# Other issuing engines for some loads and stores, and another written-out instruction order, in a fused gated recurrence and MLP kernel

## Chip, cores and metric

The kernel runs on one core of one Trainium2 chip. The metric is device time in microseconds (us) of one execution; all arithmetic is in float32 except where raw bits are moved.

## The reference

There are two parts. The first is a gated linear recurrence with batch 4, 8 heads, 768 time steps and head width 48; the second is a per-token MLP with a residual, on the heads laid side by side (384 wide).

```python
f = 1.0 / (1.0 + np.exp(-f_logit))
for t in range(S):
    state = f[:, :, t, :, None] * state + np.einsum('bhd,bhe->bhde', k[:, :, t], v[:, :, t])
    y[:, :, t] = np.einsum('bhd,bhde->bhe', q[:, :, t], state)
x = y.transpose(0, 2, 1, 3).reshape(B, S, H * D)
xn = (x - mean(x)) / np.sqrt(var(x) + 1e-06) * g_ln
out = x + np.maximum(xn @ w_ch1, 0.0) @ w_ch2        # w_ch1: 384 x 1536, w_ch2: 1536 x 384
```

## The kernel before

**Units.** The 768 steps are cut into 12 units of 64 steps, all four batches at once. A unit's 256 tokens lie as two groups g of 128 rows. Units 0 and 1 of the MLP use plain matmuls; from unit 2 the second matrix product is a seven-product block scheme (`pp`, L1025), and from unit 3 the first one is a 15-product block scheme (`by_blocks`; banks `bw`, `bx`, `bv`, `by`, `bz`, L931).

**Attention stages of a unit n**, each a token `a{n}.stage` in an order string: `gates` (sigmoid of f on ScalarE, L685 or L689), `after` and `upto` (products of gates as scans on VectorE, L658 and L670), `k` and `q` (VectorE products with the gates into `kh` and `qh`, L677 or L706 and L715), `kept` (state by total gate, L724), `carried` (L738), `scores` (L752), `causal` (mask on VectorE, L758), `kt`, `values` (L787, then copies into `x`, L796 and L798), `stats`, `norm` (L855), `turn` (transposes into `xt`, L866 and L868), `chunk` (L825) and `state` (L833).

**Transposed inputs.** Units 0 to 2 transpose f, k and q on TensorE (`tr`, L650; `kp`, L778 for kh). From unit 3 on ("direct") this is done by DMA: `split` (token `p`) packs one group of f, q, k or kh (written K) into 16-bit halves with a ScalarE copy (`planes`, L433, two buffers) and sends 256 KB of it to DRAM (`halves`, L437); `transfer` (token `x`) and `kt` bring it back with a transposing DMA issued by SyncE (L452).

**Loads.** `load` (token `l`) issues one 96 KB DMA for each batch, so four for a unit's f, k, q or v (two with a trailing group digit), on SyncE's queue (L464). Weights arrive as int64 words in 12 pieces of 768 KB: `f` issues the DMA (L526), `r` splits words on ScalarE (L538, L539), `w` rebuilds the float bits on VectorE (L547, L550, L552) and adds on GpSimd (L554). `T` and `t` mix blocks of the second matrix (L577), `u` and `U` blocks of the first (L603); capitals are on GpSimd. `d` is an idle matmul (L568).

**Order.** Nothing is scheduled by a planner. `START` is one written list for units 0 to 2 of the MLP and the attention of units 0 to 4; `UNIT` is repeated for m = 3 to 11 with n = m+1, o = m+2, p = m+3, z = m+4. Each engine and each queue executes its instructions in the order in which the list issues them. A token `m{m}` advances the MLP of unit m by one step: in a repeated unit, 15 steps of `by_blocks` and then seven `pp` products (p1, p2, p6, p5, p7, p3, p4). `s{m}` makes the block sums that p6, p5, p7 and p3 read (L910 to L913), `y{n}` those for the next unit's `by_blocks` (L901). Single PSUM banks come from a pool of four. `h00` and `h01` advance the first matrix product of unit 0 for each group (L880).

Semaphores of DMAs come from eight lanes used in turn by SyncE's and ScalarE's queues, so a DMA can wait for an earlier one in its lane to land, whichever of the two queues that one is on.

Of the kernel before, what the change touches and what calls it, by code (L numbers as in the profile page):

```python
# [299 lines left out]


START = """
l0q0 d a0.gates0 d l0k0 f a0.kx0 l0f1 a0.after0 a0.carried a0.upto0 l0q1 a0.k0 l0v0
a0.q0 r a0.gates1 l0k1 f l0v1 a0.scores0 w d a0.kx1 a0.after1 a0.causal0 a0.values0
a0.k1 f a0.upto1 d a0.stats0 f l1f f d r a0.q1 w a0.kt l1k a0.scores1 d a0.norm0
a0.causal1 r a0.turn0 a0.values1 r h00 w h00 a1.gates a0.chunk a0.stats1 d r f h00 w l1q
a0.norm1 a1.after a1.upto a1.kx a0.turn1 h01 h01 l1v w a0.state h01 h00 l2f a1.q a1.kept
r w h01 f r a1.k f l2k h00 h01 r a1.carried a1.scores a1.causal h01 f a1.values a1.kt w
f a1.stats h00 r f d a1.chunk a1.norm a2.gates d a1.turn a2.kx w r m1 m1 m1 l3f w l2v w
f r r a1.state p3f0 w w m1 a2.after l3v l2q a2.k l3k p3f1 u m0 m0 m1 p3k0 a2.upto a2.kt  # L310
a2.kept l4f T x3f m0 a2.q p3k1 m0 a2.carried U l3q x3k a2.scores U p4f1 a3.gates
a2.causal t m0 a3.after p3q0 a2.chunk a2.values U m0 p3q1 l4k a2.stats p4k0 u x3q p4f0
m1 a2.state u l5f a2.norm m1 u m1 u u a2.turn a3.k m1 a3.upto a3.q p3K0 x4f p3K1 p4k1 m2
a3.kept u l4q m2 x4k u m2 a3.carried p4q1 a4.gates t a3.kt p4q0 a3.scores m2 a4.after
l5k x4q p5f0 p5f1 m1 m2 a3.causal l4v a4.upto a4.k m2 m1 p5k0 a3.values a3.chunk s2 m2 U
a3.stats m1 m2 a4.q m2 p5k1 a3.norm x5f l5q m2 p4K1 l6f a3.turn p4K0 a5.gates a3.state
m2 l5v y3 a4.kept m2 m2 U
"""
UNIT = """
a{n}.kt a{o}.after m{m} m{m} p{o}q0 m{m} m{m} m{m} a{n}.carried p{o}q1 x{o}k a{n}.scores  # L320
a{n}.causal m{m} m{m} a{n}.values m{m} x{o}q p{p}f0 a{o}.upto m{m} l{p}k a{n}.stats m{m}
m{m} p{p}f1 m{m} m{m} a{n}.norm m{m} m{m} s{m} a{o}.q l{z}f a{n}.turn x{p}f a{n}.chunk
a{n}.state m{m} p{p}k1 m{m} m{m} p{p}k0 a{o}.k l{p}q m{m} y{n} m{m} p{o}K0 p{o}K1 m{m}
a{p}.gates l{p}v m{m} a{o}.kept
"""


# [1 line left out]
def kernel(  # L329
# [19 lines left out]
    nc = tc.nc  # L349
    B, H, S, D = q.shape  # L350
    P = 128
    T = 64
# [48 lines left out]
    for name, fill in (("f", 40.0), ("q", 0.0), ("k", 0.0)):  # L401
        t = consts.tile([P, G, H, 64], FP32, name=f"{name}raw")
# [9 lines left out]
    halved = {}  # L412

    def raw_of(n, name):

        return wide_heads["k" if n >= DIRECT and name == "q" else name]
# [3 lines left out]
    def whole(n, name):  # L420
        if name != "K":
            return raw_of(n, name)
        return by_gates[n].rearrange("p (g s) t -> p g s t", g=G)

    def split(n, name, g):

        if n >= NU or n < DIRECT:
            return
        if (n, name) not in halved:
            halved[n, name] = drams.tile([P, 2, G, 64 * H], U16, tag=f"{name}halves",  # L430
                                         name=f"{name}halves{n}")
        planes = raws.tile([P, 2, 64 * H], U16, tag="planes", name=f"{name}planes{n}_{g}")
        nc.scalar.copy(  # L433
            out=planes,
            in_=whole(n, name)[:, g].rearrange("p h e -> p (h e)").bitcast(U16).rearrange(
                "p (c two) -> p two c", two=2))
        nc.gpsimd.dma_start(out=halved[n, name][:, :, g], in_=planes)  # L437

    def transfer(n, name):

        if n >= NU or n < DIRECT:
            return
        if not turned:
            turned["k"] = wide_heads["q"].rearrange("p g h e -> p (g h e)").rearrange(
                "p (s t) -> p s t", t=T)
            turned["f"] = turned["q"] = work.tile([P, NS, T], FP32, name="turned")
        transposed(turned[name].rearrange("p (g s) t -> p g (s t)", g=G), n, name)
# [7 lines left out]
    def load(n, name, gs=range(B // 2), engines=(nc.sync,)):  # L455
        if n >= NU:
            return
        if name != "v":
            loaded[n, name] = raw_of(n, name)
        elif (n, name) not in loaded:  # L460
            loaded[n, name] = raws.tile([P, G, H, D], FP32, tag="rawv", name=f"v{n}")
        src = {"f": f_logit, "k": k, "q": q, "v": v}[name]
        for b in (b for b in range(B) if b // 2 in gs):
            engines[b % len(engines)].dma_start(  # L464
                out=loaded[n, name][(b % 2) * T:(b % 2 + 1) * T, b // 2, :, 0:D],
                in_=src[b, :, n * T:(n + 1) * T, :].rearrange("h p d -> p h d"))
# [40 lines left out]
    def pieces(dst, src, name, by_rows):  # L507
        rows, cols = dst.shape[1], dst.shape[2]
        sv = src.rearrange("(c p) f -> p c f", p=P)
        r, w = (PIECE // cols, cols) if by_rows else (rows, PIECE // rows)  # L510
        return [(f"{name}{i}_{j}", sv[:, i:i + r, j:j + w], dst[:, i:i + r, j:j + w], r, w)
                for i in range(0, rows, r) for j in range(0, cols, w)]

    queue = pieces(w1, moe_w_ch1, "w1", False) + pieces(w2, moe_w_ch2, "w2", True)
# [356 lines left out]
    def first_half(n, g):  # L871
        xt = xt_of[n]
        if n not in h_of:
            h_of[n] = work.tile([P, KF, W], FP32, tag="h", bufs=2, name=f"h{n}")
        h, tokens = h_of[n], slice(g * P, (g + 1) * P)
        for i in range(0, KF, 2):
            ph = one_bank(f"ph{n}")[:, 0:2 * P].rearrange("p (i t) -> p i t", i=2)
            for j in range(2):
                for m in range(KD):
                    nc.tensor.matmul(ph[:, j], lhsT=w1[:, m, (i + j) * P:(i + j + 1) * P],  # L880
                                     rhs=xt[:, m, tokens], start=m == 0, stop=m == KD - 1)
            nc.scalar.activation(out=h[:, i:i + 2, tokens], in_=ph, func=AF.Relu)
            yield
# [19 lines left out]
    def sums(n):  # L903

        h = h_of[n]
        a11, a12 = [h[:, i:i + KH, 0:P] for i in (0, KH)]
        a21, a22 = [h[:, i:i + KH, P:W] for i in (0, KH)]
        s1, s2, s4 = [work.tile([P, KH, P], FP32, tag=f"s{i}", name=f"s{i}_{n}")
                      for i in (1, 2, 4)]
        nc.vector.tensor_tensor(out=s1, in0=a21, in1=a22, op=ALU.add)  # L910
        nc.vector.tensor_tensor(out=s2, in0=s1, in1=a11, op=ALU.subtract)
        nc.vector.tensor_tensor(out=a21, in0=a11, in1=a21, op=ALU.subtract)
        nc.vector.tensor_tensor(out=s4, in0=a12, in1=s2, op=ALU.subtract)  # L913
        sums_of[n] = s1, s2, a21, s4
# [160 lines left out]
    def run(plan):  # L1075
        for token in plan.split():
            kind, rest = token[0], token[1:]
            if kind == "a":
                n, stage = rest.split(".")
                if int(n) >= NU:  # L1080
                    continue
                if "a" + n not in running:
                    running["a" + n] = attention(int(n))
                running["a" + n].pop(stage)()
            elif kind == "m":
                if token not in running:
                    running[token] = mlp(int(rest))
                next(running[token])
            elif kind == "l":
                if rest[-1].isdigit():  # L1090
                    load(int(rest[:-2]), rest[-2], (int(rest[-1]),))
                else:
                    load(int(rest[:-1]), rest[-1])
            elif kind == "p":
                split(int(rest[:-2]), rest[-2], int(rest[-1]))
            elif kind == "x":
                transfer(int(rest[:-1]), rest[-1])
            elif kind == "h":
                if token not in running:
                    running[token] = first_half(int(rest[0]), int(rest[1]))  # L1100
                next(running[token])
            elif kind == "s":
                sums(int(rest))
            elif kind == "y":
                if FIRST <= int(rest) < NU:
                    sums_of_x(int(rest))
            else:
                {"r": read, "w": write, "f": fetch, "t": mix, "d": idle,
                 "T": lambda: mix(nc.gpsimd), "u": mix_step,
                 "U": lambda: mix_step(nc.gpsimd)}[token]()  # L1110

    run(START)
    assert not (queue or fetched or opened)
    for m in range(3, NU):
# [49 lines left out]
```

## Time and profile before

| what | us |
|---|---|
| median of 3 runs | 446.34 (446.13 to 448.22) |
| profiled execution, its own time | 447.73 |
| span of the profiled execution | 446.0 |
| PE busy in the span | 423.2 |
| DVE, ACT, POOL busy | 338.9, 215.5, 137.6 |

PE is TensorE, DVE is VectorE, ACT is ScalarE, POOL is GpSimd, SP is SyncE; a trailing q (SPq, ACTq) is an engine's own queue of instructions that issue DMAs. PEld is the weight load that runs beside PE. A share of the span is an average over stages; the time of a stage is set by what ends last there. The span is the profile's first to last instruction; what lies around it is the difference of rows two and three.

### The profile page before, as it was taken

Reading aid. Unit: us, or ns where it says so; the run is one execution under the profiler, and the core shown is the slowest. Engines: PE = TensorE matmul, PEld = TensorE weight load, DVE = VectorE, ACT = ScalarE, POOL = GpSimd, SP = SyncE. Lnnn points to the kernel's source line nnn. Section 1 sums busy time; section 2 is a strip of 40 time slices with the busy share of each in tenths; the row PEclk is TensorE's granted clock in tenths of the full one; section 3 lists DMA queues with packets and bytes.
Section 4 is the critical chain, followed back from the end, with each engine's and each line's share of the span. In section 5 each row is a group of like instructions: output and inputs, shape, how many; then the busy total and the mean of one; then the engine's idle time right before and its main releaser. Section 6 shows DMA issues by size and latency. Waiting matters only on the chain.

```text
span 446.0 us, 12989 instructions
## 1 busy us (share of the span) xinstructions
PE 423.2 (95%) x5435; PEld 391.2 (88%) x5435; DVE 338.9 (76%) x538; ACT 215.5 (48%) x364; POOL 137.6 (31%) x171
## 2 busy tenths in 40 slices
PE   4889899599999999999999999999999999999994
PEld 2679787366878999999999999999999999999994
DVE  5899687846747788888888788788798789566461
ACT  2574856324445366465555554565564562260320
POOL 2361455913113313423422323324324205002010
PEclk9999999799999999999999999999999999999999
DMA  8998899556898998999899898899799780400101
GB/s 162 206 278 171 250 208 170 149 119 154 211 195 169 204 191 181 205 191 183 191 178 182 217 214 149 218 189 184 185 175 191 196 145 25 108 1 15 24 9 34
DMA packets 193552, 71.70 MB, mean 161 GB/s; under 512 B 179408, under 2 KB 185040, under 8 KB 193488
## 3 DMA queue, kind: packets, MB, share of 16 engines
q1 hardware_dynamic: 186480, 51.63, 63.1%
q0 software_dynamic: 5760, 18.88, 12.5%
q8 instruction: 45, 0.74, 0.8%
q10 hardware_dynamic: 1248, 0.30, 0.4%
q14 instruction: 19, 0.16, 0.1%
HBM read 28.31 MB, written 23.59 MB: 116 GB/s over the span
## 4 chain that ended last, share of the span: by engine, by line
PE 84%; DMA 5%; SPq 4%; ACT 2%; DVE 1%; issue 1%; POOL 1%; ACTq 0%
PE pp L1025 31%; PE bx L931 12%; PE by L931 9%; PE po L1006 6%; PE ph L996 5%; SPq L464 4%; PE bz L931 4%; PE py L787 3%; PE py L738 2%; PE shared L752 2%; PE shared L825 2%; PE bv L931 2%; PE bw L931 2%; PE xp L866 2%; DMA v<-in_v_dram 2%
## 5 line engine op out<-in xcount | busy, mean ns | idle before, releaser
L942 ACT ACTIVATE h<-h 128x512 f32<-128x512 f32 x45 | 28.2, 631 | 55.4 <-DVE h L939 49.5
L1025 PE MATMUL pp<-mixed,h 128*128 128x192 f32 x240 | 42.3, 326 | 0.0
L1025 PE MATMUL pp<-w,h 128*128 128x192 f32 x240 | 41.6, 329 | 0.0
L1025 PE MATMUL pp<-mixed,s 128*128 128x192 f32 x240 | 40.6, 326 | 0.0
L1025 PEld LDWEIGHTS pp<-mixed,h 128*128 128x128 f32 x240 | 39.5, 190 | 0.0
L1025 PEld LDWEIGHTS pp<-w,h 128*128 128x128 f32 x240 | 38.8, 190 | 0.7
L1025 PEld LDWEIGHTS pp<-mixed,s 128*128 128x128 f32 x240 | 39.3, 190 | 0.0
L658 DVE TENSOR_TENSOR_SCAN after<-gates,ends 128x1040 f32<-128x1040 f32 (+1 forms) x13 | 29.6, 2278 | 10.2 <-ACT gates L685 7.1
L433 ACT COPY Kplanes<-kh 128x1024 uint16<-128x1024 uint16 x18 | 18.6, 1046 | 36.0 <-DMA khalves<-kplanes 27.4
L1006 PE MATMUL po<-w,h 128*128 128x384 f32 x96 | 35.0, 514 | 0.0
L1033 POOL TENSOR_TENSOR p1x<-p,x 128x192 f32<-128x192 f32 x10 | 12.4, 1236 | 65.1 <-ACT p L1040 65.1
L996 PE MATMUL ph<-xt,w 128*128 128x256 f32 x144 | 32.3, 380 | 0.0
L939 DVE TENSOR_TENSOR h<-h,by 128x512 f32<-128x512 f32 x36 | 24.8, 688 | 8.8 <-PE by L931 3.4
L996 PEld LDWEIGHTS ph<-xt,w 128*128 128x128 f32 x144 | 27.2, 190 | 4.8 <-ACT xt L868 0.3
L437 POOL DMA_DIRECT2D qhalves<-qplanes x18 | 12.4, 696 | 55.7 <-ACT qplanes L433 55.7
L931 PE MATMUL bx<-y,v 128*128 128x128 f32 x216 | 29.4, 279 | 0.0
L1006 PEld LDWEIGHTS po<-w,h 128*128 128x128 f32 x96 | 18.9, 202 | 11.4 <-issue 1.8
L670 DVE TENSOR_TENSOR_SCAN upto<-gates,starts 128x1040 f32<-128x1040 f32 (+1 forms) x13 | 28.6, 2201 | 0.4
L437 POOL DMA_DIRECT2D fhalves<-fplanes x18 | 12.7, 703 | 52.5 <-ACT fplanes L433 52.3
L433 ACT COPY kplanes<-kraw 128x1024 uint16<-128x1024 uint16 x18 | 18.2, 1044 | 20.2 <-DMA kraw<-in_k_dram 14.3
L931 PEld LDWEIGHTS bx<-y,v 128*128 128x128 f32 x216 | 26.2, 192 | 0.5
L758 DVE TENSOR_TENSOR sc<-shared,causal 128x1024 f32<-128x1024 f32 x11 | 13.4, 1223 | 15.9 <-PE shared L752 15.9
(169 smaller groups left out, 985.8 us busy)
## 6 DMA issues: line engine op xcount, KB each, us to landing
w_0words<-in_moe_w_ch_dram SPq DMA_DIRECT2D x7, 768.0 KB, 5.4
kraw<-in_k_dram SPq DMA_DIRECT2D x48, 96.0 KB, 4.6
v<-in_v_dram SPq DMA_DIRECT2D x48, 96.0 KB, 3.7
fhalves<-fplanes POOLq DMA_DIRECT2D x18, 256.0 KB, 3.6
khalves<-kplanes POOLq DMA_DIRECT2D x18, 256.0 KB, 3.5
qhalves<-qplanes POOLq DMA_DIRECT2D x18, 256.0 KB, 4.3
Khalves<-Kplanes POOLq DMA_DIRECT2D x18, 256.0 KB, 3.2
fraw<-in_f_logit_dram SPq DMA_DIRECT2D x47, 96.0 KB, 4.1
```

The costliest lines, as they stand in the source:

```text
L433: nc.scalar.copy(out=planes, in_=whole(n, name)[:, g].rearrange("p h e -> p (h e)").bitcast(U16).rearrange("p (c two) -> p two c", two=2))
L437: nc.gpsimd.dma_start(out=halved[n, name][:, :, g], in_=planes)
L464: engines[b % len(engines)].dma_start(out=loaded[n, name][(b % 2) * T:(b % 2 + 1) * T, b // 2, :, 0:D], in_=src[b, :, n * T:(n + 1) * T, : ...
L658: nc.vector.tensor_tensor_scan(out=at["after"].rearrange(flat)[:, c0:c1][:, ::-1], data0=gt[:, c0 + 1:c1 + 1][:, ::-1], data1=ends.rearran ...
L670: nc.vector.tensor_tensor_scan(out=at["upto"].rearrange(flat)[:, c0:c1], data0=gt[:, c0:c1], data1=starts.rearrange(flat)[:, c0:c1], initi ...
L758: nc.vector.tensor_tensor(out=sc.rearrange("s r e t -> s (r e) t"), in0=at["ps"].rearrange("s r e t -> s (r e) t"), in1=causal.unsqueeze(1 ...
L931: nc.tensor.matmul(banks[bank][:, i], lhsT=right[:, i * P:(i + 1) * P], rhs=left, start=new and i == 0, stop=True, skip_group_check=True)
L939: nc.vector.tensor_tensor(out=out[to], in0=out[to], in1=bank, op=op)
L942: nc.scalar.activation(out=out[to], in_=out[to] if bank is None else bank, func=AF.Relu)
L996: nc.tensor.matmul(ph[:, j], lhsT=w1[:, m, (i + j) * P:(i + j + 1) * P], rhs=xt[:, m], start=m == 0, stop=m == KD - 1)
L1006: nc.tensor.matmul(po, lhsT=h[:, i, g * P:(g + 1) * P], rhs=w2[:, i], start=i == 0, stop=i == KF - 1)
L1025: nc.tensor.matmul(pp, lhsT=a[:, i], rhs=b[:, i], start=i == 0, stop=i == KH - 1)
```

## The change

A capital `L` issues a load on ScalarE's queue in place of SyncE's, and a capital `P` sends the packed halves from SyncE in place of GpSimd; the packing copy stays on ScalarE. In the repeated unit the loads of k and q are `L` (eight of 16 DMAs) and four of eight sends are `P`: one group each of f and K, both of k. The tokens of both lists are in a new order; their kinds and numbers are the same, nine idle matmuls included.

```diff
 START = """
-l0q0 d a0.gates0 d l0k0 f a0.kx0 l0f1 a0.after0 a0.carried a0.upto0 l0q1 a0.k0 l0v0
-a0.q0 r a0.gates1 l0k1 f l0v1 a0.scores0 w d a0.kx1 a0.after1 a0.causal0 a0.values0
-a0.k1 f a0.upto1 d a0.stats0 f l1f f d r a0.q1 w a0.kt l1k a0.scores1 d a0.norm0
-a0.causal1 r a0.turn0 a0.values1 r h00 w h00 a1.gates a0.chunk a0.stats1 d r f h00 w l1q
-a0.norm1 a1.after a1.upto a1.kx a0.turn1 h01 h01 l1v w a0.state h01 h00 l2f a1.q a1.kept
-r w h01 f r a1.k f l2k h00 h01 r a1.carried a1.scores a1.causal h01 f a1.values a1.kt w
-f a1.stats h00 r f d a1.chunk a1.norm a2.gates d a1.turn a2.kx w r m1 m1 m1 l3f w l2v w
-f r r a1.state p3f0 w w m1 a2.after l3v l2q a2.k l3k p3f1 u m0 m0 m1 p3k0 a2.upto a2.kt
-a2.kept l4f T x3f m0 a2.q p3k1 m0 a2.carried U l3q x3k a2.scores U p4f1 a3.gates
-a2.causal t m0 a3.after p3q0 a2.chunk a2.values U m0 p3q1 l4k a2.stats p4k0 u x3q p4f0
-m1 a2.state u l5f a2.norm m1 u m1 u u a2.turn a3.k m1 a3.upto a3.q p3K0 x4f p3K1 p4k1 m2
...
+a0.carried d L0f1 l0k0 a0.gates0 a0.after0 a0.upto0 l0k1 a0.kx0 a0.gates1 l0q0 f l0v0
+l0q1 a0.k0 d f r a0.after1 f d d a0.q0 l1f d a0.scores0 a0.upto1 w a0.causal0 a0.kx1 f
+a0.k1 L0v1 a0.q1 r d w f a0.scores1 a0.causal1 a0.values0 r a0.values1 f a0.kt a0.stats0
+w l1k a1.gates a0.norm0 a0.chunk r a0.turn0 a0.stats1 a0.state w a0.norm1 d l1q r d h00
+l1v h00 a1.after a0.turn1 r h00 h01 h01 a1.upto w h01 h01 f a1.q L2q f l2f d h00 a1.kx
+h00 l2v l2k a1.kept r w a1.k h01 a1.carried a1.scores f a1.causal r h01 a1.values a1.kt
+w a1.stats a2.gates a1.norm a1.chunk w a2.after f h00 l3f a1.turn r w a2.kx l3k f m1 r
+m1 P3f0 P3f1 f r a2.k a1.state P3k1 w p3k0 x3f m1 m0 w m1 m1 r w m1 L4f a2.upto L3q P3q0
+a2.kept a3.gates m0 a2.q p3q1 u m0 a3.after m0 a2.kt a2.carried P4f0 a2.scores m0 x3k
+a2.causal l4k T m0 U x3q a2.values a2.chunk m1 L3v t a2.stats l4v p4k1 U m1 P4k0 a2.norm
+U a2.turn a2.state u m1 P4f1 a3.k a3.upto u a3.q L5f P3K1 t u l4q p3K0 m2 a3.kept m2 m2
...
 """
 UNIT = """
-a{n}.kt a{o}.after m{m} m{m} p{o}q0 m{m} m{m} m{m} a{n}.carried p{o}q1 x{o}k a{n}.scores
-a{n}.causal m{m} m{m} a{n}.values m{m} x{o}q p{p}f0 a{o}.upto m{m} l{p}k a{n}.stats m{m}
-m{m} p{p}f1 m{m} m{m} a{n}.norm m{m} m{m} s{m} a{o}.q l{z}f a{n}.turn x{p}f a{n}.chunk
-a{n}.state m{m} p{p}k1 m{m} m{m} p{p}k0 a{o}.k l{p}q m{m} y{n} m{m} p{o}K0 p{o}K1 m{m}
-a{p}.gates l{p}v m{m} a{o}.kept
+m{m} m{m} m{m} a{n}.kt a{o}.after m{m} m{m} p{o}q0 a{n}.carried p{o}q1 a{n}.scores
+a{n}.causal m{m} m{m} a{n}.values m{m} a{o}.upto m{m} p{p}f1 a{n}.stats m{m} L{p}k m{m}
+m{m} x{o}k m{m} x{o}q a{n}.norm m{m} P{p}f0 m{m} a{o}.k a{n}.chunk a{n}.turn m{m} s{m}
+a{o}.q l{p}v p{o}K0 y{n} P{p}k1 x{p}f P{o}K1 l{z}f P{p}k0 m{m} a{n}.state m{m} L{p}q
+m{m} m{m} m{m} a{p}.gates a{o}.kept m{m}
 """
...
-        nc.gpsimd.dma_start(out=halved[n, name][:, :, g], in_=planes)
+        queue.dma_start(out=halved[n, name][:, :, g], in_=planes)
...
-            elif kind == "l":
+            elif kind in "lL":
+                queues = (nc.scalar if kind == "L" else nc.sync,)
...
-            elif kind == "p":
-                split(int(rest[:-2]), rest[-2], int(rest[-1]))
+            elif kind in "pP":
+                split(int(rest[:-2]), rest[-2], int(rest[-1]),
+                      nc.sync if kind == "P" else nc.gpsimd)
```

More of the change, by code (lines that the diff above doesn't have):

```diff
@@ L309 @@
-f a1.stats h00 r f d a1.chunk a1.norm a2.gates d a1.turn a2.kx w r m1 m1 m1 l3f w l2v w
-f r r a1.state p3f0 w w m1 a2.after l3v l2q a2.k l3k p3f1 u m0 m0 m1 p3k0 a2.upto a2.kt
-a2.kept l4f T x3f m0 a2.q p3k1 m0 a2.carried U l3q x3k a2.scores U p4f1 a3.gates
-a2.causal t m0 a3.after p3q0 a2.chunk a2.values U m0 p3q1 l4k a2.stats p4k0 u x3q p4f0
-m1 a2.state u l5f a2.norm m1 u m1 u u a2.turn a3.k m1 a3.upto a3.q p3K0 x4f p3K1 p4k1 m2
-a3.kept u l4q m2 x4k u m2 a3.carried p4q1 a4.gates t a3.kt p4q0 a3.scores m2 a4.after
@@ L315 @@
-l5k x4q p5f0 p5f1 m1 m2 a3.causal l4v a4.upto a4.k m2 m1 p5k0 a3.values a3.chunk s2 m2 U
-a3.stats m1 m2 a4.q m2 p5k1 a3.norm x5f l5q m2 p4K1 l6f a3.turn p4K0 a5.gates a3.state
-m2 l5v y3 a4.kept m2 m2 U
+a0.carried d L0f1 l0k0 a0.gates0 a0.after0 a0.upto0 l0k1 a0.kx0 a0.gates1 l0q0 f l0v0
+l0q1 a0.k0 d f r a0.after1 f d d a0.q0 l1f d a0.scores0 a0.upto1 w a0.causal0 a0.kx1 f
+a0.k1 L0v1 a0.q1 r d w f a0.scores1 a0.causal1 a0.values0 r a0.values1 f a0.kt a0.stats0
+w l1k a1.gates a0.norm0 a0.chunk r a0.turn0 a0.stats1 a0.state w a0.norm1 d l1q r d h00
@@ L318 @@
+U a2.turn a2.state u m1 P4f1 a3.k a3.upto u a3.q L5f P3K1 t u l4q p3K0 m2 a3.kept m2 m2
+x4f u p5f0 m2 p4q1 m2 p4q0 a3.kt a4.gates u a3.carried u x4q a3.scores a3.causal
+a4.after u a4.upto L5k m2 p5f1 m1 m1 x4k a3.values s2 a4.q a3.chunk p5k0 a3.stats m2 x5f
+P5k1 m1 m2 a3.state m2 U L5v L6f a3.norm m2 a3.turn a4.k m2 P4K0 l5q y3 U m2 p4K1 m2
+a4.kept a5.gates
 """
 UNIT = """
-a{n}.kt a{o}.after m{m} m{m} p{o}q0 m{m} m{m} m{m} a{n}.carried p{o}q1 x{o}k a{n}.scores
-a{n}.causal m{m} m{m} a{n}.values m{m} x{o}q p{p}f0 a{o}.upto m{m} l{p}k a{n}.stats m{m}
@@ L423, in whole, with split @@
         return by_gates[n].rearrange("p (g s) t -> p g s t", g=G)
-    def split(n, name, g):
+    def split(n, name, g, queue):
         if n >= NU or n < DIRECT:
@@ L1088, in run @@
                 next(running[token])
-            elif kind == "l":
+            elif kind in "lL":
+                queues = (nc.scalar if kind == "L" else nc.sync,)
                 if rest[-1].isdigit():
-                    load(int(rest[:-2]), rest[-2], (int(rest[-1]),))
+                    load(int(rest[:-2]), rest[-2], (int(rest[-1]),), queues)
                 else:
-                    load(int(rest[:-1]), rest[-1])
-            elif kind == "p":
-                split(int(rest[:-2]), rest[-2], int(rest[-1]))
+                    load(int(rest[:-1]), rest[-1], engines=queues)
+            elif kind in "pP":
+                split(int(rest[:-2]), rest[-2], int(rest[-1]),
+                      nc.sync if kind == "P" else nc.gpsimd)
             elif kind == "x":
```

## The prediction

> **What bounds the kernel now.** I read the page's busy row first, then the table of busy time by stretch, cut where TensorE's work changes, then the timeline around the one stretch that stands out.
>
> ```profile
> PE 423.2 (95%) x5435; PEld 391.2 (88%) x5435; DVE 338.9 (76%) x538; ACT 215.5 (48%) x364; POOL 137.6 (31%) x171
> ```
>
> TensorE idles 446.0 - 423.2 = 22.8 us. The table says where (stretch, its width, then PE, PEld, DVE, ACT, POOL, granted clock, DMA share, GB/s):
>
> ```profile
> 0.00:57.40 57.40, 46.96 (x702) 39.69 (x702) 46.21 (x69) 32.85 (x63) 20.18 (x27) 1.00 0.93 210
> 57.40:79.70 22.30, 22.27 (x97) 17.21 (x96) 17.59 (x19) 12.14 (x18) 13.95 (x10) 1.00 0.97 201
> 79.70:90.80 11.10, 5.87 (x17) 3.36 (x20) 8.14 (x7) 3.58 (x4) 9.39 (x7) 0.69 0.60 146
> 90.80:155.00 64.20, 63.32 (x766) 51.39 (x767) 43.37 (x71) 26.62 (x43) 17.44 (x25) 1.00 0.81 174
> 187.30:219.80 32.50, 32.50 (x469) 31.91 (x468) 27.47 (x46) 18.39 (x30) 10.51 (x14) 1.00 0.97 195
> ```
>
> The idle time is 10.4 us before 57.4, 5.2 in 79.7 to 90.8 (at a clock of 0.69), 0.9 up to 155, and 5.9 after 412.6, where the last products drain. A repeated unit, such as 187.3 to 219.8, has none: a different order cannot shorten it, only open gaps in it. All that can be won lies before 155. The timelines of PE, VectorE and GpSimd show the stall:
>
> ```profile
> 84.95 1.12 PE L650 MATMUL tr<-ident,qraw 128*128 128x128 f32 x4 [5.23 <-DVE x L1011]
> 85.86 4.92 PE L1006 MATMUL po<-w,h 128*128 128x384 f32 x8
> 92.73 2.85 PE L1006 MATMUL po<-w,h 128*128 128x384 f32 x8
> 77.26 0.69 DVE L603 TENSOR_TENSOR v<-w 128x512 f32<-128x512 f32 x1 [2.04 <-POOL w L554]
> 77.87 1.75 DVE L667 TENSOR_SCALAR total<-after 128x16 f32<-128x16 f32 x1
> 84.35 0.54 DVE L1011 TENSOR_TENSOR x<-x,po 128x384 f32<-128x384 f32 x1
> 80.61 3.01 POOL L577 TENSOR_TENSOR mixed<-w 128x384 f32<-128x384 f32 x1
> ```
>
> The second group of unit 2's q transposes needs a PSUM bank that the addition at L1011 must read first. VectorE comes to that addition late: an L603 step ahead of it waited for GpSimd's last weight piece, and L667 to L724 ran stretched beside GpSimd's L577 mixing. Afterwards eight `po` matmuls took 4.92 us instead of 2.85, at the lower clock.
>
> **The change, part by part.**
>
> *The same work.* Both lists have the same tokens, nine idle matmuls included, so TensorE's work is equal and only gaps count.
>
> *The stall.* In the changed kernel's order of instructions VectorE runs `upto`, `kept` and both `qh` products of unit 2 before the L603 step and L1011; the second q group waits for a bank that ScalarE frees; the L577 mixing on GpSimd comes only after unit 2's scores. So the three causes go. Worth 5.23 (idle) + 4.92 - 2.85 (slow `po`) + 1.12 - 0.60 (slow transposes; the first group took 0.60) = 7.8 us. What is late next: the `po` step after these transposes needs the last weight pieces, and the last one's DMA now stands on SP's queue behind two sends that wait for ScalarE's packing of f. By the rows (landing 5.4, split 0.93 and 0.91, rebuild 2.1, add 1.9), after the third and fourth f loads, I place its end near 78.5 against a need near 80.4. Then `kp` of unit 2 waits for L1011, placed at 83.1 against 84.3. Margins of 1 to 2 us: nothing is charged, but each us they miss is a us.
>
> *The opening.* Unit 0's `values` move behind the second group's scores, so the first `h00` falls from 23.8 to about 28.5. The rest of the work to unit 1's first `ph` is 12 steps of 1.34 plus transposes, attention matmuls and a filler, 11.4: 27.5 us. Packed tight it ends at 56; with the ScalarE copies before `ph` 57.2, against 57.45. I take 0; bounds -2 (the gaps of 1.41 and 1.27 gone) to +4 (the later `h00` not made up).
>
> *Eight loads per unit to ScalarE.* Six repeated units (m = 3 to 8) load. One issue takes 0.633 us by SP's median L464 row, 0.736 by the one such row on ACTq, 1.895 at most. Four make 2.5 to 2.9 us. ScalarE's datapath need not stop: the gain DMA was issued from 1.66 to 2.22 while its table load ran from 1.58 to 2.86. What follows in its queue does wait. The first four (k) now stand ahead of the last relus of `by_blocks`; in the stretch 194.8 to 206.5 ScalarE is busy 9.47 of 11.7, so 0.3 to 0.7 us do not fit, more if relus ahead run late. Behind it wait VectorE's sums `s`, for p6. `s2` was ready at 206.90, p6 began at 208.98: 2.1 us of cover. `k` of the next unit (1.22) moves ahead of `s`, where VectorE idled 0.70 for the relu: 0.5 more. 0.7 + 0.5 is inside 2.1, so 0. If issues take 1.895 each, 7.6 is placed into 2.2 free: 5.4 + 0.5 - 2.1 = 3.8 us per unit. The other four (q) stand ahead of the sigmoid of gates and the next unit's first copies, in a stretch where ScalarE is busy 5.36 of 13.3: covered, but the last of them waits in its lane for a send on SP. I charge 1.0 us over six units, near the covered end because that rests on medians; bounds 0 to 23.
>
> *Eight loads off SP, four sends onto it.* SP's issues in 187.3 to 219.8 add up to 28.9 us. Off go 8 x 0.633 = 5.1; on come four of unknown length, bounded by the weight DMAs (0.37) and output DMAs (0.6 for half of 1.2): 1.5 to 2.4, or 7.6 at 1.895. The queue is lighter by 2.7 to 3.6, or heavier by 2.5. No TensorE gap hangs on it in a unit: 0. A send blocks what stands behind it: the f transpose behind the k send, and the loads of f. That transpose already waits for VectorE's `q` at 210.20, and its gates finish 1.75 us before ScalarE's next work: 0 while the packing is done by then.
>
> *Four sends off GpSimd.* 0.68 each, an engine busy 10.5 of 32.5: 0. The next packing copy waits for a buffer either way (ScalarE waited 27.4 us for GpSimd's k sends in all).
>
> The Trainium skill, "DMA: Bandwidth & Descriptors", section "Issuing engines are not separate DMA queues", speaks against the change: loads from other engines run on the same 16 DMA engines, and only issue time is saved. By it the queue edits alone win nothing, as my terms also have it; SP's 28.9 us are the row beside it.
>
> *Sum.* Span 446.0 - 7.8 + 0 + 1.0 = 439.2. The profiled execution took 447.73, 1.73 more than its span, so a like one would take 440.9; the median is 1.39 below that execution, so **439.6 us** on the footing of the runs.
>
> **The rivals.**
>
> *The stall comes back elsewhere* (12%). The margins of 1 to 2 us above fail, by a late f packing on ScalarE holding SP's queue ahead of the last weight DMA. For it: three engines in series stand before one DMA. Against: each has some slack in the rows. Price: the 7.8 back, 445 to 447.5.
> The Trainium skill, "TensorE: Matmul & The Clock Gate", section "Part 1: The HAM clock gate", has the clock halved after an idle window of about 3.4 us. The stall of 5.23 us at 0.69 agrees with it; by it a new gap of 2 us would cost 2 us and no more.
>
> *ScalarE's queue bounds the repeated unit* (18%, slower). The place is p6's wait for `s2`, behind the k loads and the last relus. With 2 us per unit, six units add 12: 446.34 - 7.8 + 12 = 450.5. It decides from 1.7 us per unit (10.1 in all, over the 0.5% line); below 0.9 the change stays faster. For it: SP issues up to 1.895, and lane waits that tie ScalarE to SP. Against: medians leave 0.9 us of cover.
>
> *The lead is lost to transfers* (8%). The DMA share is 0.91 to 0.99 in units 155 to 349.8; units that come 8 us earlier may find inputs late. For it: that share. Against: shares go to 1.14 in one stretch, so it is no ceiling, and TensorE was not kept waiting there. 443 to 446, half faster, half same.
>
> **How the numbers follow.** The forecast has 62%: 436 to 443.5 by the opening's -2 to +4. What this kernel's measurement can tell from no change is about 0.5%, 2.2 us: faster is below 444.1, slower above 448.6. Faster 0.62 + 0.04 = 0.66; same 0.12 + 0.04 = 0.16; slower 0.18. The low end, 434, adds to the opening's gain some of the gaps before it. The high end, 449.5, takes in the returned stall and the light part of ScalarE's case; some 0.14 lies above and a few hundredths below.
>
> **What would show it.** Right: no PE wait over 2 us after unit 1's first `ph` and no slice with a lowered clock near 85; the first `bw` of unit 3 near 147 instead of 155; units of 32.3 to 32.6 us without PE idle. Wrong: PE waits for L554 or L1011 between 75 and 90 (stall back); PE `pp` waiting for `s` once per unit and unit spans above 33.5 (ScalarE); PE `py` or `shared` waiting for DMA or for `kh` and `qh` after 150 (transfers); the first L880 after 30 us (opening).

## The result and the profile after

The changed kernel takes 441.12 us in the median of 4 runs (440.39 to 441.67), the kernel before beside it 446.51 (4 runs): a ratio of 0.987, 95% interval 0.984 to 0.990. That is 5.4 us less; 6.7 were forecast. A second comparison gave 441.54 against 446.01, 0.987 (0.984 to 0.991). The profiled execution took 441.33 with a span of 439.5; 439.2 was forecast. It lies close to its median, while that of before lay 1.2 us above its own, so the spans differ by 6.5 and the medians by 5.4. The ratios here and below leave out runs over 1.5% above the fastest of the same kernel; medians and ranges take in all runs.

The page's busy row, and the table by stretch (width, then PE, PEld, DVE, ACT, POOL, clock, DMA share, GB/s), the first and the last cut at the same events as before, the second around the place of the old stall:

```profile
PE 420.8 (96%) x5435; PEld 391.9 (89%) x5435; DVE 326.9 (74%) x538; ACT 215.4 (49%) x364; POOL 102.7 (23%) x136
```

```profile
0.00:59.30 59.30, 47.41 (x703) 42.14 (x703) 44.30 (x69) 31.26 (x61) 19.37 (x27) 0.91 0.93 196
81.00:96.00 15.00, 15.00 (x252) 10.20 (x253) 10.60 (x11) 4.85 (x6) 7.20 (x7) 1.00 0.79 146
180.80:213.30 32.50, 32.50 (x468) 31.92 (x467) 26.77 (x46) 18.57 (x30) 6.35 (x10) 1.00 1.04 197
```

The stretch that held the stall has no idle time and a clock of 1.00. The opening is worse than before: 11.9 us idle in place of 10.4, and a clock of 0.91. Four events split the whole difference of the spans:

| from | to | before | after | change | forecast |
|---|---|---|---|---|---|
| 0 | first `ph` of unit 1 | 57.45 | 59.27 | +1.8 | 0 |
| that | first `bw` of unit 3 | 96.50 | 88.17 | -8.3 | -7.8 |
| that | last unit's first `bw` | 258.52 | 258.96 | +0.4 | +1.0 |
| that | end of the span | 33.5 | 33.1 | -0.4 | 0 |

The timelines of PE, VectorE and GpSimd at the place of the old stall:

```profile
80.50 1.04 PE L650 MATMUL tr<-ident,qraw 128*128 128x128 f32 x8
81.37 5.33 PE L1006 MATMUL po<-w,h 128*128 128x384 f32 x16
86.53 1.04 PE L778 MATMUL kp<-ident,kh 128*128 128x128 f32 x8
80.21 3.72 DVE L670 TENSOR_TENSOR_SCAN upto<-gates,starts 128x1040 f32<-128x1040 f32 x1
86.59 0.54 DVE L1011 TENSOR_TENSOR x<-x,po 128x384 f32<-128x384 f32 x1
79.95 1.81 POOL L554 TENSOR_TENSOR w<-w_0upper,w_0units 128x768 int32<-128x768 int32 x1 [2.23 <-DVE total L667]
```

All eight q transposes run as one block of 1.04 us with no wait ahead of them, and 16 `po` matmuls take 5.33, 2.67 for eight against 4.92 and 2.85 before. `kp` follows with no gap.

The timeline of PE in the opening, and the table for a stretch behind the first new gap:

```profile
18.31 0.88 PE L752 MATMUL shared<-qh,kh 48*64 48x64 f32 x32 [2.89 <-DVE qh L677]
22.27 1.97 PE L778 MATMUL kp<-ident,kh 128*128 128x128 f32 x8
51.95 0.99 PE L778 MATMUL kp<-ident,kh 128*128 128x128 f32 x7 [2.46 <-issue]
```

```profile
21.20:25.70 4.50, 4.46 (x48) 4.24 (x48) 4.09 (x8) 4.18 (x8) 3.56 (x4) 0.52 0.79 253
```

A rebuild of a weight piece now stands on VectorE ahead of unit 0's second `kh` and `qh`, and PE waits 2.89 us for them. Behind that gap the clock is at half: `kp` takes 1.97 us (1.04 before).

The timelines of ScalarE, its queue and PE where the last q loads meet the one slow unit, which is the first behind the units that load (it begins at 341.30 and takes 33.73 us; those ahead of it take 32.27 to 32.50):

```profile
337.81 4.74 ACTq L464 DMA_DIRECT2D kraw<-in_q_dram  x4
342.60 1.06 ACT L685 ACTIVATE gates<-turned 128x1024 f32<-128x1024 f32 x1 [4.82 <-DMA out_dram<-u4y]
344.69 1.16 PE L931 MATMUL bx<-y,w 128*128 128x128 f32 x8 [0.54 <-ACT h L936]
```

Elsewhere the four q loads take 2.67 to 2.73 us. Here the fourth comes about 2 us late; the profile names an output store from SyncE as what ended the wait, which fits a shared lane. ScalarE is idle for 4.82 us ahead of the gates, and PE waits for a copy (L936) behind them.

### The profile page after: what moved, and what is told of

Read it like the earlier page. It is cut to its first block, busy times and chain, and to the rows that moved or that the text cites. A ratio compares the mean times of both kernels' runs of the same rounds, so it can differ in the third digit from the quotient of the medians.

```text
span 439.5 us, 12938 instructions
## 1 busy us (share of the span) xinstructions
PE 420.8 (96%) x5435; PEld 391.9 (89%) x5435; DVE 326.9 (74%) x538; ACT 215.4 (49%) x364; POOL 102.7 (23%) x136
## 4 chain that ended last, share of the span: by engine, by line
PE 71%; DMA 10%; issue 5%; ACT 5%; DVE 3%; ACTq 2%; POOL 2%; SPq 2%; POOLq 0%; DVEq 0%
PE pp L1025 26%; PE bx L931 11%; PE by L931 9%; PE ph L880 4%; PE bz L931 3%; DMA fhalves<-fplanes 3%; PE py L787 2%; PE py L738 2%; PE shared L752 2%; PE tr L650 2%; ACTq L464 2%; PE ph L996 2%; DMA kraw<-in_k_dram 2%; PE bv L931 2%; PE bw L931 2%
## 5 line engine op out<-in xcount | busy, mean ns | idle before, releaser
L658 DVE TENSOR_TENSOR_SCAN after<-gates,ends 128x1040 f32<-128x1040 f32 (+1 forms) x13 | 29.6, 2279 | 6.8 <-ACT gates L685 3.8
L1006 PE MATMUL po<-w,h 128*128 128x384 f32 x96 | 32.5, 488 | 0.0
L939 DVE TENSOR_TENSOR h<-h,bx 128x512 f32<-128x512 f32 x27 | 18.3, 679 | 12.9 <-PE bx L931 12.9
L1006 PEld LDWEIGHTS po<-w,h 128*128 128x128 f32 x96 | 17.9, 190 | 10.9
L868 ACT ACTIVATE xt<-xp,gain 128x128 f32<-128x128 f32 x72 | 19.9, 375 | 11.5 <-DMA fraw<-in_f_logit_dram 10.8
L1033 POOL TENSOR_TENSOR p1x<-p,x 128x192 f32<-128x192 f32 x10 | 9.3, 931 | 67.2 <-ACT p L1040 67.2
```

The lines of the kernel that those rows point to most:

```text
L658: nc.vector.tensor_tensor_scan(out=at["after"].rearrange(flat)[:, c0:c1][:, ::-1], data0=gt[:, c0 + 1:c1 + 1][:, ::-1], data1=ends.rearran ...
L868: nc.scalar.mul(out=xt[:, m, g * P:(g + 1) * P], in_=pt[:, m], mul=gain[:, m:m + 1])
L939: nc.vector.tensor_tensor(out=out[to], in0=out[to], in1=bank, op=op)
L1006: nc.tensor.matmul(po, lhsT=h[:, i, g * P:(g + 1) * P], rhs=w2[:, i], start=i == 0, stop=i == KF - 1)
```

## The experiments

The theory: the gain is START's order, which removes the stall; the queues only have to keep up. The main rival: the queues bring the gain, or cost it, by themselves. The first four runs split the change into its parts, the next four split the queues, the last four tried to improve.

**Order alone.** Both new lists, every `L` made `l` and every `P` made `p`.

```diff
-a0.k1 L0v1 a0.q1 r d w f ...    P3f0 P3f1 ...    L{p}k ...
+a0.k1 l0v1 a0.q1 r d w f ...    p3f0 p3f1 ...    l{p}k ...
```

> Both new orders, but every load on SyncE's queue and every send on GpSimd's, as in the kernel before. Theory 'order' (the gain is the stall at 79.7 us of the kernel before, which the new order of the first units removes; the queues are worth nothing by themselves): 439.5 to 442.5 us, the first bw of unit 3 at 148 to 150 us, no PE wait over 3 us after 60 us. Theory 'queues' (a lighter SyncE queue and sends that GpSimd no longer issues are what lets TensorE go ahead): within 1 us of the kernel before, 445.5 to 447.5, or slower, because SyncE's queue gets the eight loads of a unit back in an order made for two queues; then TensorE waits appear in each repeated unit.

Measured: 453.28 us (449.15 to 457.16) beside 446.46, ratio 1.017 (1.014 to 1.021). The timeline of PE:

```profile
25.98 1.48 PE L787 MATMUL py<-v,sc 64*64 64x48 f32 x32 [5.64 <-DMA v<-in_v_dram]
207.65 4.14 PE L1025 MATMUL pp<-mixed,s 128*128 128x192 f32 x24 [0.59 <-DVE s L911]
```

The second wait recurs in three more units (1.17, 1.21, 0.82). This execution (449.15) is the fastest of the six, 4.1 us below their median, so its lines account for a part of the loss only. The theory fell in its first form: the wait for L1011 is gone here too, yet the order alone is slower than before. It needs the queues at two places, each tried by itself below.

**The stall alone.** The kernel before, with one `u` moved behind `a2.q` and `T` behind `a2.scores`.

```diff
-... p3f1 u m0 m0 m1 p3k0 a2.upto a2.kt a2.kept l4f T x3f m0 a2.q p3k1 ... a2.scores U ...
+... p3f1 m0 m0 m1 p3k0 a2.upto a2.kt a2.kept l4f x3f m0 a2.q u p3k1 ... a2.scores T U ...
```

> The kernel before with two tokens moved in its first list: the VectorE step u (L603, which waits for the last weight piece) behind a2.q, and the GpSimd mixing T behind a2.scores. Queues and all else as before. Theory 'order, by this stall': VectorE reaches L1011 near 80.0 instead of 84.4, the PE wait of 5.23 us becomes 0 to 0.6, the clock stays up, and the time is 446.5 - 7.8 = 438.7, taken as 438 to 441. Rival 'the stall only moves': the mixing collides with the next VectorE work, a wait of 3 us or more comes before unit 2's values, and the time is 443 to 447.

Measured: 444.04 us (439.49 to 448.93), ratio 0.992 (0.989 to 0.995). The timelines of VectorE, PE and GpSimd:

```profile
72.99 6.02 DVE L658 TENSOR_TENSOR_SCAN after<-gates,ends 128x1040 f32<-128x1040 f32 x1
79.86 1.25 PE L778 MATMUL kp<-ident,kh 128*128 128x128 f32 x8 [2.46 <-DVE kh L677]
73.18 3.64 POOL L554 TENSOR_TENSOR w<-w_0upper,w_0units 128x768 int32<-128x768 int32 x2
```

The wait for L1011 falls from 5.23 to 0.37 us, and the first `bw` of unit 3 comes 3.2 us earlier than before. A wait of 2.46 for `kh` takes part of the place: the scan ahead of `kh` took 6.02 us instead of 2.32, longer by 3.70, which is the 3.64 of GpSimd's two weight additions beside it. So 2.4 us (by the medians beside it) to 3.2 of the stall's 7.8 came without a new order of the rest. The time is the rival's: the stall moves in part.

**START alone, and UNIT alone.**

```diff
 START = (after's, with its L and P)   |  (before's)
 UNIT  = (before's)                    |  (after's, with its L and P)
```

> The changed kernel's list of the first units (with its queues), the repeated unit of the kernel before. Theory 'order': all of the gain and a little more, since the wait in the changed kernel's unit from 310 to 344 us (1.3 us over the others) goes too: 439 to 441.5. Rival 'the unit is needed' (the old unit cannot take over 6 us earlier, its transfers come too late): TensorE waits in the first repeated units, 443 or more.

> The first list of the kernel before, the changed kernel's repeated unit (with its queues). Theory 'order': nothing gained, and the 1.3 us of the last loading unit lost: 446.5 to 448.5, the stall at 79.7 us unchanged. Theory 'queues': 441 to 444.

Measured: START alone 441.37 us, ratio 0.990 (0.987 to 0.993); UNIT alone 447.45, ratio 1.001 (0.999 to 1.004), its stall still there with 5.68 us. The whole gain lies in START, its order and its queues together. With its own queues the new UNIT is neither better nor worse.

**Queues alone.** Before's two lists, with `L` and `P` on the loads and sends that have them after.

```diff
-... a0.upto0 l0q1 ... l0k1 f l0v1 ...   m{m} l{p}k a{n}.stats ... p{p}k1 ... l{p}q ...
+... a0.upto0 l0q1 ... l0k1 f L0v1 ...   m{m} L{p}k a{n}.stats ... P{p}k1 ... L{p}q ...
```

> The kernel before with its own two orders; the loads and sends that the change issues from ScalarE and SyncE are issued from there here too. Theory 1 (the new queues only serve the new orders: in the old order nothing that TensorE waits for stands behind a load or a send): the stall near 85 stays at 5 to 6 us, units stay at 32.3 to 32.5, and the time is within 1 us of the kernel before, 445.5 to 447.5. Rival (lighter queues help by themselves, SP being busy for 28.9 of 32.5 us): units or the stall get shorter and the time falls by 2 to 5 us, 441.5 to 444.5. Third (in the old order the first four loads on ScalarE stand ahead of the relus and delay the sums `s`): PE `pp` waits for `s`, units above 33, 450 or more.

Measured: 470.7 us (468.69 to 475.38) beside 447.18, ratio 1.056 (1.050 to 1.062). The timelines of ScalarE, its queue and PE in one unit:

```profile
236.91 3.66 ACTq L464 DMA_DIRECT2D kraw<-in_k_dram  x2
240.62 0.60 ACT L936 ACTIVATE h<-bz 128x512 f32<-128x512 f32 x1 [5.27 <-DMA qraw<-khalves]
241.27 2.08 PE L931 MATMUL bz<-y,w 128*128 128x128 f32 x8 [4.46 <-ACT h L936]
```

Two of the four k loads began 2.3 us behind the others, took 3.66 us and held the copy that reads the bank of `bz`; the profile names SyncE's transposing DMA of k as what ended that wait. Six units take 33.5 to 39.6 us, 4.5 more than 32.3 on average. This is the prediction's slower rival, in the old order, at another wait than the one it named and at more than its 2 us per unit. In ScalarE's order of the changed kernel these four loads stand one step later, behind that copy and ahead of a relu that waits for VectorE's `h` anyway: there they take 0.60 + 2.29 us, and TensorE waits for nothing behind them.

The loss lies wholly in the repeated units. Ahead of them the queues alone gain: the first `bw` of unit 3 comes at 151.19, against 153.95 in the kernel before and 152.98 in the run of UNIT alone, which has the same START as before. The timeline of GpSimd before, then those of VectorE and PE with the queues alone:

```profile
71.39 0.86 POOL L437 DMA_DIRECT2D fhalves<-fplanes  x1 [5.08 <-ACT fplanes L433]
```

```profile
78.08 0.69 DVE L603 TENSOR_TENSOR v<-w 128x512 f32<-128x512 f32 x1 [0.25 <-POOL w L554]
82.28 0.55 DVE L1011 TENSOR_TENSOR x<-x,po 128x384 f32<-128x384 f32 x1
82.88 0.66 PE L650 MATMUL tr<-ident,qraw 128*128 128x128 f32 x4 [1.75 <-DVE x L1011]
```

Before, GpSimd waited 5.08 us for ScalarE's packing of f ahead of that send, with its last two weight additions behind it, and VectorE's L603 waited 2.04 us for them. With the send on SyncE that wait is 0.25, VectorE reaches L1011 at 82.28 instead of 84.35, and PE waits 1.75 us there (and 0.79 for `qh`) in place of 5.23, also because it comes to that place 1.4 us later. So the stall has a part that the queues take away without a new order. START's queues in the old order with the old UNIT were not run.

**One kind of transfer back at a time.** The changed kernel with the unit's k loads on SyncE, with the unit's sends on GpSimd, or with unit 0's second v load on SyncE.

```diff
-L{p}k                                         +l{p}k
-P{p}f0 ... P{p}k1 ... P{o}K1 ... P{p}k0       +p{p}f0 ... p{p}k1 ... p{o}K1 ... p{p}k0
-L0v1                                          +l0v1
```

> The changed kernel; only the four k loads of the repeated unit go back to SyncE. Theory 1 (in the new order these loads stand ahead of the transposing DMAs of k and q on SyncE's queue, so `kh`, which stands ahead of the sums on VectorE, comes late; 3.5 us of issue on SP): PE `pp` waits 0.6 to 1.2 us for `s` in four or five units, VectorE waits about 2 us for `qraw` ahead of L706, units 33.1 to 33.6, time 443.5 to 446. Rival (the order of the unit with all loads on SyncE lost its 0.7 us per unit to the sends on GpSimd, not to the loads): 440.5 to 442, units 32.3.

> The changed kernel; only the four sends of the repeated unit go back to GpSimd. Theory 1 (loads, not sends, decide the unit): within 1 us of the changed kernel, 440.3 to 442.2, no PE wait for `s`. Rival (a send on GpSimd stands behind the additions of `p1x` and holds a packing buffer longer, so ScalarE packs and relus late): PE waits of 0.3 to 1 us per unit, 443 to 447.

> The changed kernel; only the v load of unit 0's second group (two DMAs) goes back to SyncE, where it stands behind two weight pieces. Theory 1 (this load alone made the 5.64 us wait of `py` in the run of the order alone): `py` of the second group starts near 26 instead of 21.2, the first `h00` near 33 instead of 28.4, the whole later by 4 to 5 us: 445 to 446.5. Rival (the lateness there came from the first f loads, which are also on SyncE in that run, or is made up by shorter gaps later): 440.5 to 443.

Measured, beside 447.18: k loads back 445.59, ratio 0.996 (0.992 to 1.000); sends back 447.23, ratio 0.996 (0.993 to 1.000); v load back 447.28, ratio 1.001 (0.998 to 1.004). Each by itself gives away most or all of the gain. The profiled execution with the sends back took 448.51, above its median, so its lines show a mechanism and not a size.

With the k loads back, the timelines of SyncE's queue, VectorE and PE:

```profile
289.57 3.52 SPq L464 DMA_DIRECT2D kraw<-in_k_dram  x4
293.14 3.54 SPq L452 DMA_TRANSPOSE qraw<-khalves  x1
300.99 1.54 DVE L706 TENSOR_TENSOR kh<-qraw,after 128x1024 f32<-128x1024 f32 x1 [3.51 <-DMA qraw<-khalves]
304.54 5.82 PE L1025 MATMUL pp<-mixed,s 128*128 128x192 f32 x24 [2.22 <-DVE s L911]
```

The loads stand 3.52 us ahead of the transposing DMA whose data `kh` needs, and the new UNIT has `kh` ahead of the sums `s`. So p6 waits, in four units by 0.2 to 2.2 us (in the one of 0.85 us the profile names a packing copy). This is theory 1 of that run.

With the sends back, the timelines of GpSimd, VectorE and PE:

```profile
180.07 0.69 POOL L437 DMA_DIRECT2D khalves<-kplanes  x1 [2.60 <-ACT kplanes L433]
181.41 0.35 DVE L1033 TENSOR_TENSOR p<-p,pp 128x192 f32<-128x192 f32 x1 [4.24 <-POOL u2x L1033]
181.82 1.16 PE L931 MATMUL bw<-y,w 128*128 128x128 f32 x8 [1.55 <-DVE p L1033]
```

Theory 1 fell. The rival's waits and time came about, but not by its mechanism: GpSimd's send waits for ScalarE's packing, the addition `u2x` waits behind the send, VectorE's next addition waits for `u2x`, and PE for the bank that it reads.

With the v load back, the timelines of SyncE's queue and PE:

```profile
18.59 1.27 SPq L464 DMA_DIRECT2D v<-in_v_dram  x2
24.67 1.38 PE L787 MATMUL py<-v,sc 64*64 64x48 f32 x32 [4.83 <-DMA v<-in_v_dram]
```

From ScalarE the same load is issued at 11.91. The first `bw` of unit 3 comes at 151.97 instead of 147.44: two DMAs on another queue carry 4.5 us of the gain (3.7 against 148.29 in the second profile of the changed kernel). In the run of the order alone the same event came at 152.09, so START's other loads and sends, moved together, are worth next to nothing there: 0.1 us.

**Tries to improve.** The first `w` behind `a0.q1` and one `r` behind `a1.kt`; the last loading unit's q loads on SyncE; both together with `a0.kt` ahead of `a0.values1`; and the changed kernel again beside them.

```diff
-a0.scores0 a0.upto1 w a0.causal0 a0.kx1 f a0.k1 L0v1 a0.q1 r d w f
+a0.scores0 a0.upto1 a0.causal0 a0.kx1 f a0.k1 L0v1 a0.q1 w r d w f
-a1.causal r h01 a1.values a1.kt w
+a1.causal h01 a1.values a1.kt r w
-L{p}q
+L{p}q, and l{p}q where m = 8
```

> The changed kernel with two tokens of START moved later: the first `w` from ahead of unit 0's second key product to behind `a0.q1`, and the `r` between unit 1's causal mask and its values to behind `a1.kt`. Theory 1 (the two new gaps of the opening, 2.89 us at 18.31 and 2.46 us before 51.95, are made by that rebuild of a weight piece on VectorE and by that split on ScalarE, which waits for its DMA ahead of the copies that free a bank): the gap at 18.3 falls to about 0.8, the one before 51.95 to under 0.5, the first `ph` of unit 1 starts at 55 to 57 instead of 59.27, and the time falls by 2 to 4 us against the changed kernel, 437 to 439.5. Rival (the weight pieces that come 2 us later are what PE waits for next): a new wait of `ph` or `po` for L552 or L554, and the time is 440 to 442.

> The changed kernel; in the last unit that loads (m = 8) the four q loads are issued from SyncE. Theory 1 (ScalarE's issues took 4.74 us there because the last of them waited in its lane for an output store, and the gates and a relu behind it came late): the unit that began at 341.30 takes 32.3 instead of 33.73, time lower by 1.0 to 1.5 us, 439.5 to 440.5. Rival (the wait goes to something else in that unit, or the difference drowns in what this kernel's time varies by): 440.5 to 442.

> The two edits above together, and unit 0's `kt` transposes moved ahead of its second group of values, into the 1.22 us for which PE waited for the one bank of `py`. Theory 1 (the gaps are apart and their gains add): 3.5 to 6 us below the changed kernel, 435 to 438. Rival (what the opening gains is lost again to the weight pieces, at `po` or in unit 2): 438 to 441, the first `bw` of unit 3 still near 147.

> The changed kernel itself once more, beside the three others and as many runs of the kernel before. Theory 1 (its gain is steady): 440.4 to 442, ratio 0.985 to 0.990. Rival (on another chip the queues, each lane tied to another queue's DMAs, run into waits that the first profile did not have, as the single edits did): 442 to 446 with units above 32.5.

Measured, beside 446.01: moved tokens 442.92, ratio 0.992 (0.989 to 0.995); q loads 440.84, 0.988 (0.986 to 0.991); all 441.36, 0.990 (0.987 to 0.994); the changed kernel 441.54, 0.987 (0.984 to 0.991). None beats it by more than can be told. The timelines of VectorE and PE with the moved tokens:

```profile
18.21 2.04 DVE L550 TENSOR_SCALAR w_256body<-w_256body 128x768 int32<-128x768 int32 x1
21.95 1.10 PE L787 MATMUL py<-v,sc 64*64 64x48 f32 x32 [5.37 <-DVE sc L764]
52.60 0.98 PE L778 MATMUL kp<-ident,kh 128*128 128x128 f32 x7 [2.26 <-issue]
```

The gap at 18.3 fell from 2.89 to 0.35 as expected, but two rebuilds then stood in a row ahead of the second causal mask, one of their steps at 2.04 us instead of 0.56 beside a GpSimd addition, and `py` waited 5.37. The `r` was not the cause of the other gap: ScalarE's copies of `x` were done at 51.6, and PE still began the same matmul only at 52.60, after 2.26 us.

The unit that took 33.73 us takes 32.27 with the edit of the q loads, but also in the second profile of the changed kernel without it, so that wait isn't steady and the edit's worth stays open. Another unit of that profile took 33.94:

```profile
237.32 4.14 PE L1025 MATMUL pp<-mixed,s 128*128 128x192 f32 x24 [1.43 <-DVE s L911]
```

There VectorE's `kh` waited 2.65 us for the transposing DMA of k, whose issue took 5.22 us instead of 2.83. The late units of the two profiles of one kernel lie at different places.

## Why the prediction held, and where it did not

- **The stall, -7.8.** Right in size: -8.3 to the first `bw` of unit 3. That it came at 147.44 where 147 was forecast is less than it looks, since before it came at 153.95 and not at 155; the prediction's own terms give 146.2. The cause was right but one step short: it left out that GpSimd's additions were late behind a send that waited 5.08 us for packing, which the change moves to SyncE, so that the queues take part in it. Its "three causes go" was too strong: GpSimd still stretched a scan, `upto` to 3.72 us, but nothing waited for it.
- **What is late next.** The last weight piece was ready at 81.76, not near 78.5. The need was misplaced as well: the `po` step began at 81.37 without waiting, so no rival arose. L1011 ran at 86.59, not 83.1, and `kp` ran from 86.53 without a gap. The margins were right only in what they decided.
- **The opening, 0 within -2 to +4.** It cost 1.8, inside the bounds: 1.45 more idle time and 0.45 more busy time. The first `h00` came at 28.44 (28.5 forecast). The failed step is the sum of work "packed tight": it left no room for VectorE's rebuild ahead of `kh`, nor for the clock. The low bound is mis-added as well: 439.6 - 2 is 437.6, not 436.
- **Loads on ScalarE, +1.0.** The units took 0.4 more than before. The four k issues took 2.7 to 3.2 us and the four q issues 2.7, at or a little over the 2.5 to 2.9 forecast, with 4.74 once. The step "0.7 + 0.5 is inside 2.1, so 0" held in every unit of this profile; in the second one p6 waited for `s` in two units (1.43 and 0.30 us), the longer wait behind SyncE's queue and not ScalarE's. The "1.895 at most" is the maximum of the f row alone: the v row of the same view has 2.871.
- **Sends, 0.** On SyncE 0.55 to 0.61 us each in the repeated units, 2.3 for four, as bounded.
- **"The queue edits alone win nothing".** This is the step that the runs correct most. The Trainium skill, "DMA: Bandwidth & Descriptors", section "Issuing engines are not separate DMA queues", says that another issuing engine saves only issue time. No run disputes that the transfers share their engines, but the queue decided what stood behind what: +24 us with the old order, 4.5 us for one v load with the new one. The prediction had 23 us as its upper bound for the loads and took 0 to 1; it never priced START's `L0v1`. In START the queues even gained by themselves, up to 2.8 us. The time came out right because order and queues came together.
- **The clock.** The prediction drew from the Trainium skill, "TensorE: Matmul & The Clock Gate", section "Part 1: The HAM clock gate", that a new gap of 2 us costs 2 and no more. Behind a gap of 2.89 us, with 0.63 us of work in the 3.5 us around it, the clock was 0.52 to 0.56 for 7.4 us; after the gap of 2.46 it was 0.65 for 3.1. The measurement decides: a gap below 3 us can also lower it. Not each does: 2.22 us ahead of 304.54 with the k loads back was followed by 0.51 for 3.5 us, 2.46 ahead of 79.86 in the run of the stall alone by 1.00.

That the spans agree within 0.3 us is in part luck: the four rows of the table miss by +1.8 and by -0.5, -0.6 and -0.4, which nearly cancel.

Of the rivals, the returned stall did not occur. ScalarE's queue as bound did not occur in the changed kernel beyond one unit of +1.5 us, yet the run of the queues alone shows that it was the real danger and what kept it away: in the new order the loads stand one step later on ScalarE. Lost to transfers: a DMA share of 1.04 in a unit without idle PE speaks against it.

## What to carry to other kernels

Moving a DMA to another queue is a change of order: look at what stands behind it on the new queue, at what it stood ahead of on the old one, and at whose semaphore lane it shares, and test queue and order together, since here the order alone was 1.7% slower than no change and the queues alone 5.6%, though the latter gained in the first units. When a stall is removed, read the next instruction of each engine at that place, above all a VectorE step that now falls beside a GpSimd one. A wait that one profile shows once, such as that behind the last q loads, should be looked for in a second profile before an edit is made for it.

## What was not expected of the hardware

- Three VectorE steps beside a GpSimd weight addition grew by about the time that they shared with it: the scan L658 from 2.32 to 6.02 us beside 3.64, `upto` from 2.33 to 3.72 where 1.55 of an addition overlapped it, L550 from 0.56 to 2.04 beside 1.62. In the changed kernel a scan that began 0.23 us ahead of the addition kept its 2.32 and the addition grew from 1.8 to 3.71; the scan of 6.02, by the profile, also began ahead, by 0.19, so the recorded starts do not say which of the two waits. Not every step grows: in the kernel before, two `kh` products (L677) ran beside such additions in 1.29 us, as `qh` does in the changed kernel with none beside it (1.27). The Trainium skill, "SBUF — State Buffer", section "SBUF: two separate sides", calls the port pair of these two an exclusive lock held for a whole instruction; these sums agree with that.
- PE waits 0.90 to 2.95 us behind the first `kp` matmul of unit 1 in every run with the new START, always at that matmul, with nothing in the profile that released it; before, it waits 1.41 us three matmuls later, and in the three other runs with the old START 1.16 to 2.15 there, where the profile names ScalarE copies. Moving a split on ScalarE away left it. Its cause is open.
- ScalarE issues DMAs while its datapath works: a k load was issued from 192.63 to 193.23 while the copy of `bz` ran from 192.67 to 193.27.
